# Batch by batch: an attention block and two gated MLPs on one core, with the spatial mix of the first batch moved between the attention tiles of the second

## The chip, the cores and the metric

The kernel runs on one core of a Trainium2 chip. The metric is the device time of one execution in microseconds; three runs before the change gave 393.71, 396.62 and 400.88 us, a median of 396.62 us. One execution was profiled: it took 399.25 us, of which the trace spans 396.5 us.

The engines are named as the profile names them: PE (TensorE matmul) and PEld (its weight loads), DVE (VectorE), ACT (ScalarE), POOL (GpSimd) and SP (SyncE, which here only issues DMAs). Each works through its own list of instructions in the order of that list.

## The reference

Two batches of 768 positions go through three stages. Chunked attention (8 heads of 64, chunks of 32 with 16 positions to the left, 8 to the right and 8 memory slots) gives `x` (2 x 768 x 512). A gated MLP mixes along the positions. A second MLP has a three-tap convolution along the positions.

```python
scores = q_c @ k_full.T / 8; a = softmax(scores); x = a @ v_full        # per chunk of 32
h = gelu(x @ w_in); u, v = h[..., :512], h[..., 512:]
v_n = (v - mean) / sqrt(var + 1e-6) * g_ln
v_s = einsum('ts,bsd->btd', w_sg, v_n) + b_sg[None, :, None]            # mixes positions
x2 = x + (u * v_s) @ w_out
h = relu(x2 @ w_in2)
conv = sum over k of conv_w[k] * h shifted by k - 1 positions
out = (h * sigmoid(conv)) @ w_out2
```

## The kernel before, in words

Every large product is done with fp16 halves: each operand is scaled by a power of two and split into a high and a low part, and `mm3` (line 155) sums three fp16 matmuls (high x high, high x low, low x high) in one PSUM bank. The scale comes from a bound: ACT sums absolute values (`abs_sum`, line 133), `top_of` (lines 116 to 118) transposes the sums on PE, takes their maximum on DVE, and spreads it over the partitions with a matmul against ones; `scale_from` (lines 124 and 126, DVE) makes the power of two, and `split` cuts the high part on ACT (line 141) and the low part on DVE (line 147) or POOL (lines 144 and 145). Weights arrive as 64-bit floats and are first narrowed on DVE (`narrow`, lines 103, 105 and 107).

The work is written as tokens in two strings, FIRST and SECOND; each letter is a step and its number a tile or block:

- `q i` scores of attention tile i (line 258; 12 tiles of 128 positions, six for each batch) and row maxima; `e g` the exponential of a group of tiles (line 279); `b i` transposes the weights (pp, line 285), copies them (ptr, line 288), multiplies with the values (pv, line 296), normalizes into `xx` (line 312) and bounds the result; `x i` transposes `xx` (px, line 328) and splits it.
- `c`, `s`, `k` narrow, bound and cut the eight blocks of `w_in`; `V i` and `U i` are the two halves of the first MLP (vps and ups); `N g` normalizes three tiles of v; `S` loads the mixing weights.
- `M n` is a block of the mix (group n // 4 of 384 positions; groups 0 and 1 are batch 0), `O n` the product with `w_out`, `I n` the product with `w_in2`, the convolution and the gate (n // 8 is the batch), `G b` and `H n` bound and split the gates of a batch, `Y n` the last product and the store.
- `J n` takes n jobs from a queue that holds the cutting of the later weights.

A scheduler then places the instructions on PE, DVE, ACT and POOL within the limits of buffers and data; SP keeps the order in which the program is written. Buffers come from pools: the attention's SBUF pool `at` and its PSUM pool are given back when FIRST has ended (`p1.close()`), and only then is the staging pool `st2` for the later weights opened. One `q` load has 256 KB, one tile of keys 2 x 256 KB, one of values 2 x 260 KB, and a block of `w_in` 512 KB.

## Time and profile before

| | |
|---|---|
| median of three runs | 396.62 us |
| the profiled execution, its span | 399.25 us, 396.5 us |
| busy PE, DVE, ACT, POOL | 336.8, 239.1, 218.5, 81.8 us |
| mean granted clock of TensorE | 0.914 |
| HBM read and written | 33.29 and 3.15 MB |

A busy PE is one with a matmul under way, at whichever clock was granted: 1.00 is 2.4 GHz, 0.50 is 1.2 GHz. A stretch that is busy at a lower clock holds less work than its busy time says.

### The profile page before, as it was taken

To read this page: it belongs to the slowest core of one execution; us is meant where nothing else is said; L and a number is where in the kernel's file an instruction comes from. 1 tells how busy PE (TensorE), PEld (TensorE's weight loads), DVE (VectorE), ACT (ScalarE), POOL (GpSimd) and SP (SyncE) were. 2 spreads that over 40 slices of the span, in tenths; PEclk is the share of its full clock that TensorE was granted. 3 is DMA by queue.
4 is the path that set the end of the run, shared out by engine and by line. 5 is a ranking of instruction groups with operands and counts; after the bars stand their busy time and mean duration, and the time that the engine had idled before them with its cause. 6 is when DMAs were issued, how large, how long until landed. Compare 5 with 4: busy or idle time off the path is not lost.

```text
span 396.5 us, 7270 instructions
## 1 busy us (share of the span) xinstructions
PE 336.8 (85%) x2890; PEld 211.7 (53%) x2890; DVE 239.1 (60%) x467; ACT 218.5 (55%) x439; POOL 81.8 (21%) x204
## 2 busy tenths in 40 slices
...
GB/s 221 294 312 187 159 57 211 249 105 163 119 68 69 70 0 8 194 160 2 21 144 48 108 106 2 114 100 0 3 106 0 2 54 26 28 26 28 26 79 53
DMA packets 14161, 36.89 MB, mean 93 GB/s; under 512 B 2352, under 2 KB 2608, under 8 KB 14128
## 3 DMA queue, kind: packets, MB, share of 16 engines
...
q8 instruction: 22, 0.36, 0.4%
q14 instruction: 11, 0.09, 0.1%
HBM read 33.29 MB, written 3.15 MB: 92 GB/s over the span
## 4 chain that ended last, share of the span: by engine, by line
PE 48%; DVE 17%; DMA 17%; ACT 10%; issue 4%; POOL 2%; SPq 1%; ACTq 0%; DVEq 0%; POOLq 0%
PE o L155 22%; PE i L155 7%; PE mx L155 5%; PE ups L155 4%; DMA raw<-in_w_out_dram 4%; PE vps L155 4%; DMA rvXF<-in_w_in_dram 3%; DMA ruWSG<-in_w_in_dram 3%; DMA kwb<-in_kw_dram 3%; PE sc L258 2%; DMA sgUF<-in_w_sgt_dram 2%; DVE c L690 2%; PE pv L296 2%; PE px L328 1%; ACT h L686 1%
## 5 line engine op out<-in xcount | busy, mean ns | idle before, releaser
L155 PE MATMUL o<-wp,gsp 128*128 128x512 f16 (+1 forms) x312 | 66.0, 371 | 6.9 <-ACT gsp L141 6.9
L155 PE MATMUL i<-x2s,wi 128*128 128x384 f16 x384 | 67.1, 332 | 0.2 <-ACT h L686 0.2
L155 PEld LDWEIGHTS <-wi 128*128 128x128 f16 x384 | 38.2, 100 | 27.8 <-issue 3.6
L155 PEld LDWEIGHTS <-gsp 128*128 128x128 f16 x312 | 30.9, 99 | 39.8 <-ACT gsp L141 8.0
L155 PE MATMUL mx<-wsg,vs 128*128 128x384 f16 x288 | 50.8, 333 | 0.0
L155 PE MATMUL vps<-win,xs 128*128 128x512 f16 x144 | 36.8, 400 | 4.1 <-ACT xs L141 3.8
L155 PEld LDWEIGHTS <-vs 128*128 128x128 f16 x288 | 28.3, 99 | 19.6 <-issue 2.3
L155 PE MATMUL ups<-xs,win 128*128 128x128 f16 x576 | 38.6, 225 | 0.0
L155 PEld LDWEIGHTS <-win 128*128 128x128 f16 x576 | 35.7, 101 | 4.5 <-issue 1.4
L155 PE MATMUL o<-gs,wo 128*128 128x384 f16 x192 | 34.5, 326 | 0.8 <-ACT gs L141 0.7
L690 DVE SCALAR_TENSOR_TENSOR c<-h,cw_sb,c 128x768 f32<-128x768 f32 x16 | 16.2, 1015 | 17.1 <-ACT c L689 17.1
L155 PEld LDWEIGHTS <-wo 128*128 128x128 f16 x192 | 18.5, 98 | 11.9 <-issue 0.2
L155 PEld LDWEIGHTS <-xs 128*128 128x128 f16 x144 | 13.3, 102 | 21.5 <-ACT xs L141 4.6
L361 DVE BATCH_NORM_STATS2 st<-v 128x6 f32<-128x512 f32 x12 | 8.3, 690 | 23.0 <-ACT v L359 23.0
L694 ACT ACTIVATE c<-c 128x768 f32<-128x768 f32 x16 | 13.4, 840 | 12.8 <-DVE c L692 12.8
L695 DVE TENSOR_TENSOR gate<-h,c 128x768 f32<-128x768 f32 x16 | 15.3, 955 | 8.5 <-ACT c L694 8.5
L720 ACT ACTIVATE o<-o,ixp0t 128x256 f32<-128x256 f32 x12 | 5.6, 469 | 21.8 <-issue 18.2
L133 ACT ACTIVATE gs<-uf 128x384 f16<-128x384 f32 x16 | 8.3, 519 | 16.3 <-DVE uf L652 13.8
L692 DVE SCALAR_TENSOR_TENSOR c<-h,cw_sb,c 128x768 f32<-128x768 f32 x16 | 16.2, 1015 | 0.7
L677 POOL MEMSET h<- 128x1 f32 x16 | 2.0, 129 | 68.0 <-DVE gate L695 64.2
L258 PE MATMUL sc<-kwa,q 128*32 128x128 f32 x192 | 7.9, 300 | 9.3 <-DMA kwa<-in_kw_dram 7.3
L391 POOL TENSOR_TENSOR vs<-v,vs 128x512 f16<-128x512 f32 x12 | 14.0, 1190 | 7.7 <-ACT vs L390 7.7
...
## 6 DMA issues: line engine op xcount, KB each, us to landing
...
```

The costliest lines, as they stand in the source:

```text
L133: nc.scalar.activation(room, src, AF.Abs, scale=2.0 ** (1 - EXP_TOP), accum_out=acc)
L155: nc.tensor.matmul(ps, a, b, start=(i == 0), stop=(i == n - 1))
L258: nc.tensor.matmul(sc[c * CH:(c + 1) * CH, hp].rearrange("p (a k) -> p a k", a=2), q_t[i][:, hp, c * CH:(c + 1) * CH], kw_t[i][:, :, hp, c ...
L296: nc.tensor.matmul(po[c * CH:(c + 1) * CH, hp // 2, (hp % 2) * PW:(hp % 2 + 1) * PW] .rearrange("p (a k) -> p a k", a=2), t[:, hp, c * CH: ...
L328: nc.tensor.transpose(pp[:, k * P:(k + 1) * P], x[:, k * P:(k + 1) * P], ident)
L361: nc.vector.bn_stats(out=st, in_=v)
L391: nc.gpsimd.tensor_tensor(out=lo[:, ib, :], in0=v, in1=hi[:, ib, :], op=ALU.subtract)
L690: nc.vector.scalar_tensor_tensor(out=c, in0=h[:, 0:S], scalar=cw_sb[:, f, 0:1], in1=c, op0=ALU.mult, op1=ALU.add)
L692: nc.vector.scalar_tensor_tensor(out=c, in0=h[:, 2:S + 2], scalar=cw_sb[:, f, 2:3], in1=c, op0=ALU.mult, op1=ALU.add)
L694: nc.scalar.activation(c, c, AF.Sigmoid)
L695: nc.vector.tensor_tensor(out=gate[b][f // 4][:, f % 4], in0=h[:, 1:S + 1], in1=c, op=ALU.mult)
L720: nc.scalar.activation(o[:, cs], ps[:, cs.start - cols.start:cs.stop - cols.start], AF.Copy, scale=inv_of(sc_g["gate", b], f"t{b}", f"p{h}"))
```

## The change

FIRST is reordered and a third string, B1, is added for the second batch. Its main points:

- **Loads.** Loads are tokens now (`A` q, `D` keys, `R` values, `W` blocks of `w_in`); the first tile's values, then the four blocks of the v half of `w_in`, stand ahead of tile 1.
- **Mix of batch 0.** M0 to M7 stand in B1, between the attention tiles of batch 1, and `w_out` is loaded and cut there too (`T`, into buffers outside `st2`). In SECOND the blocks of O, M and I are mixed.
- **Steps split.** `p` (pp and ptr) is taken out of `b`; `h` (the first half of a tile's bound) out of `b` and its second half goes to `x`; U is done in two halves (`u`, `w`). Scores stand some tiles ahead of their use. The groups of the exponential have one or two tiles instead of up to three.
- **Bounds in two steps.** `top_a` does the transpose and the maximum, `top_b` the matmul against ones. All bounds share one PSUM bank (`tops`, three places in turn); the spare columns of that bank take dummy matmuls (`Z`), of which there are 180 in place of 70.
- **Buffers.** Scores have one PSUM bank, pp and px two (before: four for all and for bounds), ptr has one buffer in place of two. Some low parts that POOL cut (four tiles of x, two blocks of `w_out2`) go to DVE.
- **End.** Four of the blocks of batch 0's last product, Y2 to Y5, stand after the last `I`, ahead of the second batch's product; before, Y5 alone did.

```diff
-PX = (4, 9, 10, 11)
-PK = ('p1',)
-SPMAN = True
-XBUFS, SBUFS, QBUFS, PTBUFS = 2, 2, 2, 2
+PK = ()
+QBUFS, PTBUFS, SBUFS = 2, 1, 2
 RAWBUFS = 2
-LOADS = "q0 q1 wv0 v0 wv1 v2 v1 wu0 wu1"
-GROUPS = ((0,), (1,), (2, 3), (4, 5), (6, 7, 8), (9, 10, 11))
+GROUPS = ((0,), (1,), (2,), (3, 4), (5, 6), (7, 8), (9, 10), (11,))
+SG = max(len(g) for g in GROUPS)
...
-Z q0 e0 c0 q1 e1 c1 b0 c2 c3 s0 q2 q3 e2 x0 k0 k1 k2 k3 b1 x1 c4 c5 V0 c6 c7 s1 b2 V1 x2 k4 k5 k6 k7 q4 q5 e3
-b3 V2 x3 U0 b4 V3 U1 x4 S U2 b5 V4 N0 x5 U3 q6 q7 q8 e4 V5 J2 U4 b6 J2 U5 N1 J2 x6 J2 b7 x7 J2 V6 b8 x8 U6
-V7 q9 q10 q11 e5 U7 V8 b9 x9 U8 N2 b10 x10 V9 b11 x11 U9 V10 U10 V11 U11 N3
+A0 D0 R0 W0 W1 W2 W3 A1 D1 R1
+Z70 q0 e0 A2 D2 R2 W4 W5 W6 W7 c0 p0 c1 Z30 b0 R3 c2 c3 Z60 h0 s0 x0 o0 k0 k1 k2 k3 q1 e1 A3 D3 Z20 V0 p1 q2 e2 A4 D4 b1 R4 c4 c5 p2 h1 b2 R5 c6 c7 x1 q3 A5 D5 V1 h2 s1 q4 e3 A6 D6 x2 o1 k4 k5 k6 k7 p3 U0 b3 R6
+q5 A7 D7 S0 S1 S2 V2 q6 e4 A8 D8 h3 u1 x3 p4 w1 b4 R7 J1
+V3 N0 h4 J1 u2 x4 p5 w2 b5 R8 J1
+q7 A9 D9 V4 J1 q8 e5 A10 D10 h5 u3 x5 p6 J1 w3 b6 R9 J1
+J1 V5 h6 J1 u4 x6 p7 w4 J1 b7 R10 J2
+"""
+B1 = """
+q9 A11 D11 V6 N1 q10 e6 h7 u5 x7 p8 w5 M0 b8 R11
+V7 h8 M1 u6 x8 p9 w6 b9 M2
+q11 e7 V8 h9 M3 u7 x9 p10 w7 b10 M4 g0
+V9 N2 h10 r0 T u8 x10 p11 w8 b11 M5 J1
+V10 J1 h11 M6 u9 x11 w9 J1
+V11 J1 N3 u10 J1 M7 w10 J1
+U11 g1 J3
...
 SECOND = """
-J1 M0 J1 M1 J1 M2 J1 M3 J1 M4 J1 M5 J1 M6 J1 M7 J1 M8 J1 O0 J1 M9 J1 O1 J1 M10 J1 O2 J1 M11 J1 O3 J1 M12 J1 O4 J1
-M13 J1 O5 J1 M14 J1 O6 J1 M15 J1 O7 J1 O8 J1 O9 J1 O10 J1 O11 J1 O12 I0 O13 J1 O14 I1 O15 J1 I2 J2 I3 J2 I4 J2 I5
-J3 I6 J3 I7 J3 G0 I8 H0 H1 H2 H3 I9 H4 H5 H6 H7 I10 Y0 I11 Y1 I12 Y2 I13 Y3 I14 Y4 I15 Y5 G1 H8 H9 H10 H11 H12 H13 H14
-H15 Y6 Y7 Y8 Y9 Y10 Y11
+M8 J1 r1 M9 J1 O0 J1 O1 J1 O2 J1 O3 J1 M10 J1 a0 O4 J1 O5 d0 O6 J1 O7 J1 M11 J1 a1 M12 J1 g2 d1 M13 J1 r2 J3 I0 J1 I1 M14 J1 I2 M15 J1 I3 J1 O8 g3 O9 J1 O10 r3 J1 O11 J1 I4 a2 O12 J1 O13 d2 J1 I5 O14 J1 O15 J1 I6 a3 J1 I7 d3 J1
+I8 G0 J1 I9 K0 J1 H0 H1 J1 I10 H2 H3 J2 I11 H4 H5 J2 I12 H6 H7 J2 I13 J9 Y0 I14 Y1 I15 Y2 G1 Y3 K1 H8 H9 Y4 H10 H11 Y5 H12 H13 H14 H15 Y6 Y7 Y8 Y9 Y10 Y11
...
+    pst = ctx.enter_context(tc.tile_pool(name="pst", bufs=1, space=bass.MemoryType.PSUM))
+    pst_t = pst.tile([P, 512], F32, tag="top", name="tops")
+    top_ps = pst_t[:, :3 * P + 3].rearrange("p (n c) -> p n c", n=3)
+    idle_ps = pst_t[:, 3 * P + 3:]
+    tops = [0]
...
-    small = [lambda name: ps1.tile([P, 512], F32, tag="a", name=name, bufs=4)]
-
-    def small_ps(name):
-        return small[0](name)
...
-    def top_of(m, name, ones=None):
+    def top_a(m, name):
 
         n = m.shape[1]
-        t = small_ps(name + "t")
+        tops[0] += 1
+        t = top_ps[:, tops[0] % 3]
         r = sm.tile([P, 1], BF16, tag="red", name=name + "r", bufs=4)
         nc.gpsimd.memset(r, 2.0 ** -120)
         nc.tensor.transpose(t[:n, 0:P], m, ident)
         nc.vector.tensor_reduce(out=r[:n], in_=t[:n, 0:P], axis=AX.X, op=ALU.max)
-        nc.tensor.matmul(t[:, 256:257], ones_bf if ones is None else ones, r, start=True, stop=True)
-        return t[:, 256:257]
+        return t, r
+
+    def top_b(tr, ones=None):
+
+        t, r = tr
+        nc.tensor.matmul(t[:, P:P + 1], ones_bf if ones is None else ones, r, start=True, stop=True)
+        return t[:, P:P + 1]
...
     def qk(i):
-        sc = sc_t[i] = small_ps(f"sc{i}").rearrange("p (h k) -> p h k", h=4)
+        sc = sc_t[i] = ps1.tile([P, 512], F32, tag="sc", name=f"sc{i}", bufs=1).rearrange("p (h k) -> p h k", h=4)
         for hp in range(4):
             for c in range(4):
                 nc.tensor.matmul(
...
                     kw_t[i][:, :, hp, c, :],
                     start=True, stop=True,
                 )
-        load_qk(i + 2)
...
+        pp = ps1.tile([P, 512], F32, tag="a", name=f"pp{i}", bufs=2)
...
-        if i in PX:
-            nc.scalar.copy(xf[b][:, :, ts], ppv)
-        if i in sc_x:
-            split(xs[b][0][:, :, ts], xs[b][1][:, :, ts], ppv, sc_x[i], xf[b][:, :, ts] if i in PX else None)
-        if i not in PX:
-            nc.scalar.copy(xf[b][:, :, ts], ppv)
+        split(xs[b][0][:, :, ts], xs[b][1][:, :, ts], ppv, sc_x[i])
+        nc.scalar.copy(xf[b][:, :, ts], ppv)
...
+    def u_pe(i, part):
         b, ib = divmod(i, KS)
         sl = slice(ib * P, (ib + 1) * P)
-        ps = ps_t["u", i] = mmps1(f"ups{i}").rearrange("p (j q) -> p j q", j=KD)
-        for j in range(KD):
+        if part == 0:
+            ps_t["u", i] = mmps1(f"ups{i}").rearrange("p (j q) -> p j q", j=KD)
+        ps = ps_t["u", i]
+        for j in (2 * part, 2 * part + 1):
...
+                if n == 0:
+                    raw_t["o"] = big.tile([P, 2, DM], src.dtype, tag="WI1", name="rawo")
+                raw_t[n] = raw_t["o"][:, n % 2:n % 2 + 1]
+            else:
+                raw_t[n] = late_pool[0].tile([P, ks.stop - ks.start, cs.stop - cs.start], src.dtype, tag="raw",
+                                             name=f"raw{n}", bufs=RAWBUFS)
...
+    def warm(n):
+
+        for _ in range(n):
+            nc.tensor.matmul(idle_ps, ones_bf, ones_bf[:, :idle_ps.shape[1]], start=True, stop=True)
...
+    def bound(kind, g):
+        acc_t[kind, g] = top_a(acc_t[kind, g], f"{kind}{g}")
+
+    def scaled(kind, g):
+        sc_g[kind, g] = scale_from(top_b(acc_t.pop((kind, g))), f"{kind}{g}")
...
+    def wo_jobs():
+        def get():
+            late["wo"] = [big.tile([P, KD, DM], F16, tag=t, name=f"wo{t}") for t in ("WO0", "WO1")]
+            return late["wo"]
+
+        stage_jobs("o", w_out, KD, slice(0, DM), get)
+        issue(0)
+        issue(1)
+
+    steps["M"] = lambda n: mix(n // KD, n % KD)
+    steps["T"] = lambda n: wo_jobs()
+    steps.update({
+        "g": lambda n: bound("gs", n), "r": lambda n: scaled("gs", n), "a": lambda n: bound("x2", n), "d": lambda n: scaled("x2", n)})
+    run(B1)
+    p1.close()
+    late_pool.append(ctx.enter_context(tc.tile_pool(name="st2", bufs=1)))
+    tp = ctx.enter_context(tc.tile_pool(name="tp", bufs=2))
+    ps2.append(ctx.enter_context(tc.tile_pool(name="ps2", bufs=7 - PS_MM, space=bass.MemoryType.PSUM)))
```

Three places on PE. First, what stands ahead of V0 (`vps_463` before, `vps_464` in the change); sc, px, pp and pv are an attention tile's scores, transposes and products, wvt and tops the bounds, and a wait names the engine or DMA queue it is for. Before:

```order
L118 MATMUL wvt<-wvr,ones_bf 128x1 [waits DVE_49]
L258 MATMUL sc_337<-kwa,q_233 32x128 [waits DMAHW6_49,DMAHW7_49,DMAHW0_49,PE_49]
...
L258 MATMUL sc_362<-kwb,q_263 32x128 [waits DMAHW2_49,DMAHW3_49,DMAHW1_49,PE_49]
...
L328 MATMUL px_387<-ident,xx 128x128 [waits DVE_49]
...
L285 MATMUL pp_406<-ident,s_269 128x128 [waits DVE_49]
...
L155 MATMUL vps_463<-win_107,xs_307 128x512
```

Now:

```order
L343 MATMUL px_395<-ident,xx 128x128 [waits DVE_49]
...
L273 MATMUL sc_492<-kwa,q_232 32x128 [waits DMAHW6_49,DMAHW0_49,DMAHW7_49,DVE_49,PE_49]
...
L125 MATMUL tops<-ident,wav 4x128 [waits DVE_49]
L299 MATMUL pp_485<-ident,s_437 128x128 [waits Activation_49]
...
L310 MATMUL pv_518<-vwSTG,ptr_490 32x130 [waits DMAHW5_49,DMAHW4_49,Activation_49]
...
L132 LDWEIGHTS ones_bf [waits DVE_49]
L132 MATMUL tops<-wvr,ones_bf 128x1 [waits Pool_49]
L299 MATMUL pp_551<-ident,s_511 128x128 [waits PE_49,Activation_49]
...
L533 MATMUL tops<-ones_bf 128x125 [waits DVE_49]
```

V0 stood behind the scores of tiles 2 and 3 (`sc_337`, `sc_362`); now it stands behind those of tile 2 alone (`sc_492`), tile 1's product with the values, the bound of the weights and 20 dummies. The transpose for the weights' bound (`wav`), whose data ACT makes, now also waits for DVE.

Second, PE around V7 in batch 1. Before, between the product with the values of tile 8 and the next transpose stood V and U alone:

```order
L296 MATMUL pv_1468<-vwSTG_95,ptr_1466 32x130 x16
...
L155 MATMUL vps_1563<-win_107,xs_1266 128x512
...
L155 MATMUL ups_1649<-xs_1266,win_107 128x128
...
L116 MATMUL xt8t<-ident,xa_1491 1x128
L328 MATMUL px_1502<-ident,xx 128x128 x4
L258 MATMUL sc_1583<-kwb,q_1129 32x128 x16
```

Now:

```order
L310 MATMUL pv_1642<-vwSTG_98,ptr_1587 32x130 x7
...
L169 MATMUL mx_0_1618<-wsg_820,vs_1018 128x384
...
L169 MATMUL vps_1667<-win_112,xs_1307 128x512
...
L343 MATMUL px_1743<-ident,xx 128x128 x4
L299 MATMUL pp_1751<-ident,s_1464 128x128 x2
L125 MATMUL tops<-ident,xa_1663 1x128
...
L169 MATMUL mx_1_1691<-wsg_820,vs_1018 128x384
...
L169 MATMUL ups_1714<-xs_1307,win_112 128x128
```

A block of the mix (18 matmuls, `mx_0`, `mx_1`) now stands between a tile's product and its transposes, and another between its transposes and U.

Third, PE at the end, from the last `I` (i_7 of batch 1) to batch 1's first block of the last product (`o_0_0_4055` before, `o_0_0_4127` in the change). Before:

```order
L155 MATMUL i_7_3976<-x2s_2952,wi_2512 128x384
...
L155 MATMUL o_5_0_3997<-wp_3007,gsp_3520 128x512
...
L116 MATMUL gt1t<-ident,gacc_3526 16x128
L118 LDWEIGHTS ones_low
L118 MATMUL gt1t<-gt1r,ones_low 128x1
...
L155 MATMUL o_0_0_4055<-wp_3007,gsp_4034 128x512
```

Now:

```order
L169 MATMUL i_7_3962<-x2s_3173,wi_2621 128x384
...
L169 MATMUL o_2_0_3983<-wp_3242,gsp0XS_3634 128x512
...
L125 MATMUL tops<-ident,gacc_3545 16x128
...
L169 MATMUL o_3_0_4016<-wp_3242,gsp0XS_3634 128x512
...
L132 MATMUL tops<-gt1r,ones_low 128x1
...
L169 MATMUL o_4_0_4057<-wp_3242,gsp0XS_3634 128x512
...
L169 MATMUL o_0_0_4127<-wp_3242,gsp1XS_4048 128x512
```

One block of 24 matmuls stood between the last `I` and the gates' bound; now four blocks stand between the last `I` and batch 1's last product, one ahead of each step of the bound and two behind it.

## Rows read from the trace of the kernel before

**Rows 1.** Stretches: length, busy PE, PEld, DVE, ACT, POOL, SP; clock; DMA share; GB/s

```profile
0.00:41.40 41.40, 18.23 (x247) 14.91 (x248) 24.40 (x47) 12.53 (x28) 19.55 (x31) 0.65 0.92 252
41.40:104.00 62.60, 52.35 (x729) 38.92 (x730) 28.69 (x75) 37.86 (x58) 14.41 (x50) 0.93 0.59 156
104.00:172.00 68.00, 55.40 (x681) 39.19 (x680) 33.10 (x81) 36.38 (x62) 17.95 (x48) 0.87 0.26 74
172.00:293.00 121.00, 120.01 (x778) 72.84 (x777) 103.15 (x208) 78.59 (x192) 20.58 (x51) 1.00 0.21 70
293.00:312.00 19.00, 11.65 (x55) 5.72 (x53) 17.62 (x24) 17.05 (x32) 8.15 (x10) 0.73 0.00 0
312.00:353.00 41.00, 41.00 (x216) 21.02 (x215) 21.14 (x22) 21.14 (x45) 0.80 (x12) 1.00 0.09 33
353.00:361.00 8.00, 6.04 (x29) 2.69 (x28) 4.34 (x7) 4.90 (x9) 0.33 (x2) 0.99 0.08 33
361.00:396.50 35.50, 32.17 (x166) 16.42 (x164) 6.68 (x8) 10.04 (x18) 0.00 (x0) 0.95 0.12 45
```

**Rows 2.** Timeline up to V0: start, us, engine, line, operation; idle time before it

```profile
16.32 1.96 PE L296 MATMUL pv<-vwa,ptr 128*32 128x130 f32 x32 [0.98 <-ACT ptr L288]
...
25.54 0.43 DVE L103 TENSOR_SCALAR tuVS<-ruWSG 128x512 int32<-128x512 int32 x1 [2.47 <-DMA ruWSG<-in_w_in_dram]
...
29.23 1.66 POOL L144 TENSOR_SCALAR tvXS<-tvXS,wvs 128x512 f32<-128x512 f32 x1
...
34.64 1.94 PE L258 MATMUL sc<-kwa,q 128*32 128x128 f32 x32 [7.34 <-DMA kwa<-in_kw_dram]
...
34.87 2.79 POOL L145 TENSOR_TENSOR win<-tvXS,win 128x512 f16<-128x512 f32 x2
...
37.55 1.94 PE L258 MATMUL sc<-kwb,q 128*32 128x128 f32 x32 [0.97 <-DMA kwb<-in_kw_dram]
...
41.38 3.72 PE L155 MATMUL vps<-win,xs 128*128 128x512 f16 x12
```

**Rows 3.** Waits of the attention stage and of bounds: engine, line, waited for

```profile
PE pv L296 <- ACT ptr L288: 7.4, 7, 2.0
PE xt0t L116 <- ACT xs L133: 5.6, 1, 5.6
PE xt0t L118 <- DVE xt0r L117: 2.5, 1, 2.5
PE wp1t L118 <- DVE wp1r L117: 1.7, 1, 1.7
PE gt1t L118 <- DVE gt1r L117: 0.7, 1, 0.7
```

**Rows 4.** Groups by line: busy us, mean ns of one, idle time before

```profile
L650 DVE SCALAR_TENSOR_TENSOR mt<-mx,gsc,b_sb 128x384 f32<-128x384 f32 x16 | 9.6, 607 | 1.5 <-POOL vs L391 0.9 <-PE mx L155 0.6
L652 DVE TENSOR_TENSOR uf<-mt,uf 128x384 f32<-128x384 f32 x16 | 9.1, 568 | 0.1
L528 PE MATMUL warm<-zero 128*128 128x128 f16 x70 | 6.4, 278 | 1.0 <-DVE zero L525 1.0
L279 ACT ACT_TABLE_LOAD x4 | 5.1, 1283 | 0.8 <-PEq L796 0.7
```

**Rows 5.** Timeline: the mix at full clock, and the gates of both batches

```profile
184.83 7.80 PE L155 MATMUL mx<-wsg,vs 128*128 128x384 f16 x47
...
304.89 1.03 PE L155 MATMUL o<-wp,gsp 128*128 128x512 f16 x2 [5.64 <-ACT gsp L141]
...
360.15 7.52 DVE L147 SCALAR_TENSOR_TENSOR gsp<-gate,gt1s,gsp 128x768 f16<-128x768 f32 x8 [0.81 <-ACT gsp L141]
360.18 33.00 PE L155 MATMUL o<-wp,gsp 128*128 128x512 f16 x168 [1.22 <-ACT gsp L141]
```

**Rows 6.** Chain that ended last: start, us, what; the batch-1 block in between

```profile
339.78 3.90 PE i L155 x24
343.68 5.18 PE o L155 x24
```

More of the change, by code (lines that the diff above doesn't have):

```diff
@@ L232, in fused_kernel, with load_q @@
     q_t, kw_t, vw_t = {}, {}, {}
+    def load_q(i):
+        q_t[i] = at.tile([P, 4, P], F32, tag="q", name=f"q{i}", bufs=QBUFS)
+        nc.sync.dma_start(q_t[i], qt[i])
     def load_halves(t, src):
@@ L432, in fused_kernel, with sg_load @@
     sg_t = []
-    def sg_load():
-        wsg.extend(halves("wsg", ("WSG0", "WSG1"), KS, S))
-        for tag, ks in (("UF1", slice(0, 2)), ("UF1", slice(2, 4)), ("VS10", slice(4, 6))):
-            if ks.start != 2:
-                t = big.tile([P, 4 if tag == "UF1" else 2, S], F32, tag=tag, name=f"sg{tag}")
-            sg_t.append(t[:, ks.start % 4:ks.start % 4 + 2])
-            nc.sync.dma_start(sg_t[-1], blocks(w_sgt)[:, ks])
+    def sg_load(n):
+        if n == 0:
+            wsg.extend(halves("wsg", ("WSG0", "WSG1"), KS, S))
+            t = big.tile([P, 4, S], F32, tag="UF1", name="sgt0")
+            sg_t.extend((t[:, 0:2], t[:, 2:4]))
+        elif n == 2:
+            sg_t.append(big.tile([P, 2, S], F32, tag="VS10", name="sgt2"))
+        nc.sync.dma_start(sg_t[n], blocks(w_sgt)[:, 2 * n:2 * n + 2])
+        if n == 2:
+            nc.sync.dma_start(g_sb, g_ln.rearrange("(k p) -> p k", p=P), allow_slow_non_contiguous=True)
+            nc.sync.dma_start(b_sb, b_sg.unsqueeze(0).to_broadcast([P, S]))
+            nc.sync.dma_start(cw_raw, conv_w)
+            sg_jobs()
     def sg_jobs():
```

175 lines of the change are left out of this document (58 added, 117 removed).

## The prediction

> **What bounds the kernel now.** I read the stretches first [rows 1]. PE is busy 336.8 of 396.5 us, so the question is where it is not, and there are four such places. Up to 41.4 us it waits for the first data and does 18.23 us at clock 0.65. From 41.4 to 172, the attention with the first MLP, it is busy 52.35 of 62.6 and 55.40 of 68.0 us at clocks 0.93 and 0.87. From 172 to 293 it is gapless at full clock. Around 293 to 312, the first batch's gates, it has 11.65 of 19 at 0.73, and around 353 to 361, the second batch's gates, 6.04 of 8. So there are two kinds of loss, idle time and the slower clock that goes with it. I count both: length less busy time times clock is 13.9 + 19.8 = 33.7 us in the attention stage, of which 10.25 + 12.6 = 22.9 is plain idle, and 10.5 us at the first gates. Matmul records can be missing and a mean clock covers idle time too, so I take 27 for the attention stage, between 22.9 and 33.7.
>
> Whose fault the idle time is, the waits say [rows 3]. Seven products with the values wait for ACT's copy of the weights (7.4 us), and one bound waits 5.6 us for ACT. No engine is full there: in the two halves DVE has 28.69 and 33.10 us and ACT 37.86 and 36.38 [rows 1]. PE is held by the latency of each tile's chain over ACT and DVE, with too little other work in its list between the links. Work put between the links is therefore free, as long as ACT and DVE keep up.
>
> **Start: -5 us (between -8 and +3).** V0 starts at 41.38 and runs 3.72 [rows 2], so it ends at 45.1. Ahead of it PE waits for the keys of tile 2 until 34.64 and of tile 3 until 37.55 [rows 2]. Ahead of tile 2's keys came three q, keys and values and all of `w_in`: 3 x 256 + 3 x 512 + 3 x 520 + 8 x 512 = 7960 KB. Now it is three q and keys, two values and four blocks: 768 + 1536 + 1040 + 2048 = 5392 KB. At the stretch's 252 GB/s [rows 1] the old amount takes 32.3 us, so the first 2.3 us are empty, and the new amount lands at 2.3 + 21.9 = 24.2. Tile 3's keys are no longer ahead of V0 at all. What is late next is the weights. Their three pieces on POOL, subtract 1.66 and narrow 2.79 for two, ran from 29.23 to 34.87 + 2.79 = 37.66 [rows 2], 8.4 us. In the new order the weights' bound on PE stands behind scores of tile 2 (1.94), tile 1's transposes and its products with the values (1.96) [rows 2], and on DVE behind the first narrowing of the u half (at 25.54 before). I let the bound end at 31, a little later than the 29.23 of before; POOL ends at 39.4, and V0, which takes pieces as they come, at 40. If the bound comes at 29 or earlier it is -8; if tile 2's exponential holds the list, +3. The 20 dummies directly ahead of V0 end before POOL's first piece: 110 more dummies at 6.4 / 70 = 0.091 us each [rows 4] are 10 us of PE, all before V0 where PE has 41.4 - 18.2 = 23.2 us idle. Cover gone, the last 20 would cost 1.8.
>
> **Attention stage: -17 us (between -28 and -7).** Eight blocks of the mix move here. 47 matmuls took 7.80 us [rows 5], so a block of 18 takes 2.99 and eight take 23.9. They leave the gapless stretch, where each of their microseconds counted in full, and stand where PE is idle. The DVE work of a block, 0.607 + 0.568 [rows 4], is 9.4 us for the eight, and the load, narrowing and cutting of `w_out` come too. U in halves and scores emitted tiles ahead give more pieces to put between the links. Against it: one score bank and one ptr buffer in place of shared four and two, so the next scores wait for the exponential that reads the bank, and the next copy for the last product. If ACT's 74.2 us of this stage [rows 1] stay (a few copies change), it has room in what remains, but not everywhere. The loss was 27; all of it filled leaves about 6 for the clock after short waits, the chain's waits halved leaves 16; I take 10, nearer the low end since the blocks stand at the links that waited. The ends are 6 - 33.7 and 16 - 22.9.
>
> **First gates: -6.5 us (between -9.6 and 0).** PE waits 5.64 us for the first split [rows 5], and the clock falls. Eight splits take DVE 7.52 us in the second batch [rows 5]. Before, three blocks I of 3.90 [rows 6] stood between the bound and the last product, 11.7 us; now five, 19.5. The 7.8 us more would remove most of 10.5. But DVE was busy 103.15 of 121 and then 17.62 of 19 [rows 1], and when 23.9 us of PE and only 9.4 of DVE leave, DVE has 93.8 against PE's 96. I keep 4 lost.
>
> **Second gates: -4 us (between -4 and -1).** The idle part is 8 - 6.04 = 1.96 [rows 1]. The last 168 matmuls take 33.00 [rows 5], while six blocks at 5.18 [rows 6] are 31.1: 1.9 of slow clock. Now three blocks, 15.5 us, stand behind the bound's start in place of none; the eight splits take 7.5 and the bound 1 to 2. Both items go.
>
> **Added: +2 us (between 0 and +10).** Four to five more table loads, as groups of the exponential get smaller: the order has 13 for 9, four at 1.283 [rows 4], 5.1 us of ACT, hidden in its slack of 130.6 - 74.2. Six cuts that POOL did go to DVE (a wider one, of 768 columns, takes 7.52 / 8 = 0.94 there [rows 5], so 5.6 us at most), four of them in this stage, where DVE is busy 61.8 of 130.6. Cover gone in either, the whole amount counts.
>
> **Sum:** -5 - 17 - 6.5 - 4 + 2 = -30.5. The profiled execution took 399.25 and its span 396.5, so 2.75 lie outside, and that stays. 399.25 - 30.5 = 368.75; this execution is 2.6 above the median, from which it would be 366.1. I say **367 us**.
>
> **Rivals.** *PE gapless after V0 (352 us).* Busy time times clock after 41.4 adds up to 303.0 over the rows [rows 1]; V0 would start 5 earlier at 36.4, 3.3 follow the last matmul (360.18 + 33.00 to 396.5 [rows 1, 5]), 2.75 lie outside: 345.4, and 6.7 more since I took 27 for 33.7. For it: all four losses are addressed. Against: every link still passes two engines.
>
> *The attention stage loses as much as before (384).* One score bank and one ptr buffer tie the tiles more closely than two and four did; the seven waits for ptr [rows 3] would become a wait in nearly every tile. The 17 do not come. Against it: the blocks of the mix depend on no tile of batch 1.
>
> *DVE bounds the second half (376).* DVE's 93.8 + 17.62 + 1.5 for cuts from POOL are 113 before the first gates' splits end, PE's part 96 + 11.65 x 0.73 = 104.5. Then 8.5 are lost where I kept 4, and the later splits and bounds, which queue on DVE, lose as much again: +9. For it: DVE is at 85% before, and PE's part shrinks more. Against: `w_out`'s narrowing leaves too.
>
> *Slower: the shared bank of the bounds.* All 30 bounds now use one PSUM bank. Each step on it, transpose and product, waits for DVE to have read the step before, and behind it stands all of PE's list. The order shows it: the weights' transpose, whose data come from ACT, now also waits for DVE. PE's second steps waited for the maximum 2.5, 1.7 and 0.7 at most [rows 3], the others no longer than the last, so 0.16 on average over 30 if those three were all; at that price 60 steps are 10, partly already paid. The most expensive row, 2.5, would give 150. At 0.36 us per step the gain is within 2% (367 + 21.6 = 388.6); from 0.63 per step, 37.8 us, it is slower (404.8). For it: DVE is loaded, and its list is in order. Against: the other half of the change puts other work between the two steps, so that the maximum is long done. The Trainium skill, *PSUM — Partial Sum Buffer*, section "PSUM bank collisions raise a hardware error", says to guard PSUM by semaphores by bank (and by quadrant of partitions), not by address: by that rule three places in one bank do not make three bounds independent. No row of before shows a bank shared by bounds in this way, and by that rule alone this rival stands and has its waits, not its price.
>
> **Numbers.** Forecast 0.58, gapless 0.13, DVE 0.13, attention unchanged 0.08, shared bank 0.08 (half of it within 2%, half slower). The forecast's own terms spread by about 10 either way. 8 in 10 lie from 351, the gapless case, to 387, which takes in DVE and the unchanged attention. 2% of 396.62, about what a measurement here tells from no change, puts "same" at 388.7 to 404.6. The shared bank and the tails of the two middle rivals give 0.07 same and 0.05 slower; the rest, 0.88, is faster.
>
> **What would show it.** V0 starts at 36 to 38 with POOL as its last wait; the keys of tile 2 land near 24. From V0 to the first O, PE idles 12 us or less, at a clock above 0.95. M0 to M7 have no waits of their own. No gap over 3 us at the first split of batch 0, none at the second batch's last product. I am wrong if ACT or DVE is over 90% busy in the attention stage with PE idle (the chain, not the fill, bounds), if steps on the bounds' bank (L125, L132) head PE's waits with more than 10 us, or if V0 starts after 41.

## The result, and the profile after

The changed kernel takes **380.5 us** (median of 378.60, 378.82, 382.17 and 383.01), the kernel before 397.9 beside it: a ratio of 0.960, 95% interval 0.948 to 0.972. It is faster by 17 us, where 30 were forecast; the range (351 to 387) holds it. Its profiled execution is the one of 383.01 us, with a span of 381.2, at the upper end of its runs as that of before was of its own, so spans are compared with spans: 15.3 us less.

Busy time by stretch (columns as in [rows 1]), of the kernel before, cut at other times than there:

```profile
42.00:96.00 54.00, 44.71 (x618) 31.95 (x617) 25.02 (x68) 33.62 (x55) 11.89 (x37) 0.96 0.58 156
96.00:119.00 23.00, 18.56 (x229) 14.93 (x230) 12.44 (x29) 14.96 (x23) 6.36 (x20) 0.78 0.39 101
119.00:168.00 49.00, 39.87 (x544) 29.07 (x543) 21.19 (x57) 23.60 (x39) 14.11 (x41) 0.91 0.24 67
```

The same stretches of the changed kernel:

```profile
42.00:96.00 54.00, 42.33 (x541) 29.12 (x540) 27.44 (x67) 36.57 (x54) 10.48 (x32) 0.84 0.62 167
96.00:119.00 23.00, 19.85 (x320) 15.31 (x323) 14.77 (x37) 16.57 (x25) 5.75 (x22) 1.00 0.45 107
119.00:168.00 49.00, 46.02 (x465) 30.68 (x460) 32.90 (x76) 26.28 (x57) 10.10 (x35) 1.00 0.24 77
```

Busy time times clock is the work done at full speed. From 119 to 168 it rises from 36.3 to 46.0 us: that is where the blocks of the mix now stand. From 96 to 119, before the first of them, it rises too, from 14.5 to 19.9. From 42 to 96, the first batch's attention, it falls from 42.9 to 35.6; PE is busy only 2.4 us less there, and the rest is the granted clock, 0.84 for 0.96. The change loses at the start of the stage and wins behind it.

Summed up from the start in pieces of 6 us, without the dummies, this gives the work done by a time, and the difference of two kernels is a lead that can be followed. Three of the experiments below have the changed kernel's order on every engine until well past 192 us (tail put back, cuts on POOL, spread splits) and a fourth (less narrowing) until about 165, so their profiles repeat its first half. I call these four the siblings:

```
work done (us at full clock) by     42    72    96   120   144   168   192   240   288
kernel before                      7.4  29.9  50.7  65.8  84.6 101.7 124.9 172.7 220.1
changed kernel                    12.9  32.7  49.2  70.0  94.0 115.0 136.5 183.9 229.4
  its lead                        +5.5  +2.8  -1.5  +4.2  +9.4 +13.3 +11.6 +11.2  +9.3
same first half, tail put back    14.3  35.4  52.6  74.8  98.8 119.2 142.0 189.4 233.6
same first half, spread splits    12.7  34.3  52.1  74.7  98.7 119.3 141.7 189.0 233.1
same first half, cuts on POOL     14.3  35.2  54.3  76.8 100.8 121.4 143.8 191.2 236.3
same first half, less narrowing   13.6  34.5  52.2  72.5  96.5 117.3 141.3 188.7 236.7
mix put back                      13.7  34.6  52.1  73.3  93.1 109.4 133.4 180.8 226.3
```

The profiled execution of the changed kernel is behind the four siblings, by 5 to 7 us of work at 192. The pattern is the same in all: 5 to 7 ahead at 42, most of that gone at 96, then 13 to 20 at 168.

Some of what PE waits for in the changed kernel, engine and line, then us in total, times, longest (answers to [rows 3]):

```profile
PE pv L310 <- ACT ptr L302: 6.7, 3, 4.4
PE sc L273 <- DMA kwb<-in_kw_dram: 4.9, 3, 2.1
PE tops L132 <- DVE wp1r L126: 3.2, 1, 3.2
PE tops L125 <- DVE x23s L138: 2.2, 1, 2.2
PE i L169 <- ACT h L663: 1.4, 1, 1.4
```

The wait for ptr comes three times instead of seven, and is hardly shorter in sum (6.7 us for 7.4). The places, from PE's timeline (start, us, engine, line, operation; idle time before it), for [rows 2] and [rows 5]:

```profile
40.12 0.59 PE L169 MATMUL vps<-win,xs 128*128 128x512 f16 x2 [0.49 <-POOL win L159]
...
72.89 1.96 PE L310 MATMUL pv<-vwSTG,ptr 128*32 128x130 f32 x32 [4.41 <-ACT ptr L302]
...
119.35 2.45 PE L169 MATMUL mx<-wsg,vs 128*128 128x384 f16 x14
...
302.58 0.18 PE L132 MATMUL tops<-wp1r,ones_bf 128*128 128x1 bf16 x1 [3.24 <-DVE wp1r L126]
304.15 3.61 PE L169 MATMUL i<-x2s,wi 128*128 128x384 f16 x12 [1.39 <-ACT h L663]
307.60 2.75 PE L169 MATMUL o<-wp,gsp0XS 128*128 128x512 f16 x12
```

V0's last piece ends at 40.7. The largest gap of the first batch is at 68 to 73 us, and the first block of the mix starts at 119. The first gates still cost a gap, at 299 to 304; the second batch's product follows the first's at 346.6 without one (PE is busy in all of the 70.31 us from 307.60 on, as a row below shows).

From V0's start to the first O, of the kernel before and of the changed one (columns as above):

```profile
41.38:199.41 158.03, 134.98 (x1606) 95.24 (x1606) 81.42 (x198) 86.95 (x153) 38.93 (x117) 0.92 0.38 104
34.27:192.46 158.19, 136.18 (x1621) 93.55 (x1619) 99.45 (x224) 95.04 (x172) 39.85 (x114) 0.95 0.45 121
```

The stretch is as long as before, and PE idles 22.0 us in it for 23.1.

### The profile page after: what moved, and what is told of

It reads as the page before. It is cut to its first block, busy times and chain, and to the rows that moved or that the text cites. A ratio compares the mean times of both kernels' runs of the same rounds, so it can differ in the third digit from the quotient of the medians.

```text
span 381.2 us, 7494 instructions
## 1 busy us (share of the span) xinstructions
PE 338.9 (89%) x3000; PEld 214.9 (56%) x3000; DVE 241.9 (63%) x472; ACT 221.8 (58%) x445; POOL 63.5 (17%) x192
## 4 chain that ended last, share of the span: by engine, by line
PE 55%; DMA 18%; DVE 14%; ACT 4%; POOL 3%; SPq 2%; issue 2%; ACTq 0%; DVEq 0%; POOLq 0%
PE o L169 25%; PE i L169 10%; PE mx L169 7%; PE vps L169 4%; DMA kwb<-in_kw_dram 3%; DMA cw_raw<-in_conv_w_dram 3%; DMA raw<-in_w_in_dram 3%; DMA rvXF<-in_w_in_dram 3%; DMA kwa<-in_kw_dram 2%; PE ups L169 2%; PE sc L273 2%; PE pv L310 2%; DMA q<-in_qt_dram 2%; SPq L256 2%; DMA raw<-in_w_out_dram 1%
## 5 line engine op out<-in xcount | busy, mean ns | idle before, releaser
L169 PEld LDWEIGHTS <-vs 128*128 128x128 f16 x288 | 27.2, 98 | 20.6 <-issue 1.9
L169 PE MATMUL o<-gs,woWO 128*128 128x384 f16 x192 | 32.4, 326 | 0.0
L169 PEld LDWEIGHTS <-woWO 128*128 128x128 f16 x192 | 18.6, 98 | 12.1
L402 POOL TENSOR_TENSOR vs<-v,vs 128x512 f16<-128x512 f32 x12 | 15.0, 1259 | 10.8 <-ACT vs L401 10.8
L169 PE MATMUL o<-wp,gsp1XS 128*128 128x512 f16 (+1 forms) x84 | 16.7, 349 | 0.0
L169 PE MATMUL o<-wp,gsp1VS 128*128 128x512 f16 (+1 forms) x84 | 16.7, 349 | 0.0
L169 PE MATMUL o<-wp,gsp0VS 128*128 128x512 f16 x72 | 16.7, 379 | 0.0
L169 PE MATMUL o<-wp,gsp0XS 128*128 128x512 f16 x72 | 16.5, 379 | 0.0
L310 PE MATMUL pv<-vwSTG,ptr 128*32 128x130 f32 x256 | 11.2, 312 | 5.2 <-ACT ptr L302 5.1
L283 DVE TENSOR_REDUCE mx<-sc 128x8 f32<-128x512 f32 x12 | 8.2, 687 | 11.9 <-PE sc L273 11.8
```

The lines of the kernel that those rows point to most:

```text
L169: nc.tensor.matmul(ps, a, b, start=(i == 0), stop=(i == n - 1))
L283: nc.vector.tensor_reduce(out=mx, in_=scv, axis=AX.X, op=ALU.max)
L310: nc.tensor.matmul(po[c * CH:(c + 1) * CH, hp // 2, (hp % 2) * PW:(hp % 2 + 1) * PW] .rearrange("p (a k) -> p a k", a=2), t[:, hp, c * CH: ...
L402: nc.gpsimd.tensor_tensor(out=lo[:, ib, :], in0=v, in1=hi[:, ib, :], op=ALU.subtract)
```

## The experiments

Each starts from the changed kernel. Ratios are to the kernel before, run beside them, with the 95% interval in brackets. Each version's interval is about 0.8% either way, so a difference of 3 us or less between two versions is told by the rows of their profiles or not at all. Diffs show the changed pieces of a line; `...` and `/` stand for what is left out.

**Load order undone.**

```diff
-... q0 e0 A2 D2 R2 W4 W5 W6 W7 c0 ...
+... q0 e0 W4 W5 W6 W7 A2 D2 R2 c0 ...
```

> The changed kernel with one thing undone: the four blocks of the u half of w_in stand ahead of tile 2's q, keys and values again. Theory (the new load order is worth about the 4.5 us by which V0 ends earlier): tile 2's keys land 2048 KB / 252 GB/s = 8.3 us later, at 33 to 34 us in place of 25.6; V0 ends at 45 or later in place of 40.65; the whole takes 4 to 6 us more, about 385. Rival (what V0 gains is lost again in the first batch's attention, whose chains end when the later loads and ACT let them): V0 ends later but the first block of the mix starts at about the same 119 us; the whole takes 380 to 382.

Measured: 382.6 us, 0.967 (0.959 to 0.975). From PE's timeline, the scores of tile 3, V0's last piece and the first block of the mix:

```profile
38.63 1.07 PE L273 MATMUL sc<-kwb,q 128*32 128x128 f32 x30 [2.04 <-DMA kwb<-in_kw_dram]
...
41.67 0.60 PE L169 MATMUL vps<-win,xs 128*128 128x512 f16 x2
...
120.21 2.92 PE L169 MATMUL mx<-wsg,vs 128*128 128x384 f16 x17 [0.59 <-ACT uf L418]
```

V0 ends at 42.3 and not at 45. Tile 2's scores run 6.5 us later than in the change (32.05 for 25.59), but seven of V0's twelve matmuls are placed around them, from 33.9 to 36.5. The last five stand behind the scores of tile 3, for whose keys PE waits until 38.63; POOL's pieces were done at 37.45. So V0's end hung on keys here, but on tile 3's. The mix starts 0.9 later than in the changed kernel, and the 2 us are within what the runs scatter. The rival is nearer, and the load order is worth at most these 2.

**The mix put back.**

```diff
-... w5 M0 b8 / h8 M1 u6 / b9 M2 / h9 M3 u7 / b10 M4 g0 / h10 r0 T / b11 M5 J1 / h11 M6 u9 / J1 M7 w10 / U11 g1 J3 ...
+... w5 b8 / h8 u6 / b9 / h9 u7 / b10 / h10 T / b11 J1 / h11 u9 / J1 w10 / U11 J3 ...
-M8 J1 r1 M9 ...
+M0 M1 M2 M3 M4 g0 M5 r0 M6 M7 g1 M8 J1 r1 M9 ...
```

> The changed kernel with M0 to M7 (and the bounds and splits of their two groups) put back behind the attention, ahead of M8; the load and cutting of w_out stay in the attention. Theory (the blocks fill idle time of batch 1's attention, 119 to 192 us, which lost about 5 us with them and 19.8 in the kernel before without): idle time of PE in the second half of the attention rises by 10 to 15 us, and the whole takes 390 to 395. Rival (the finer order of the other steps has closed those gaps by itself, and the blocks could stand anywhere): the stage gets shorter by the 24 us of the blocks, the rest longer by the same, and the whole stays at 379 to 382.

Measured: 387.7 us, 0.979 (0.973 to 0.986), 7 more than the change; its four runs (387.06 to 388.25) lie above all of the change's. The stretches, columns as above:

```profile
96.00:119.00 23.00, 20.20 (x310) 15.50 (x307) 16.48 (x41) 17.20 (x26) 6.82 (x23) 1.00 0.42 106
119.00:168.00 49.00, 39.76 (x437) 28.78 (x435) 29.70 (x75) 27.76 (x54) 11.08 (x33) 0.93 0.31 99
```

Work from 119 to 168 is back at 37.0, near the 36.3 of before: the finer order closed no gap there, the blocks did. From 96 to 119 it is 20.2 without any block, for 14.5 before: that part of the gain is not the mix's. So filling is the largest single part of the gain that an experiment shows, 7 of 17 us, though below the 10 to 15 that I put on it.

**The tail put back.**

```diff
-... I13 J9 Y0 I14 Y1 I15 Y2 G1 Y3 K1 H8 H9 Y4 H10 H11 Y5 H12 ...
+... I13 J9 Y0 Y1 I14 Y2 Y3 Y4 I15 Y5 G1 K1 H8 H9 H10 H11 H12 ...
```

> The changed kernel with Y2 to Y4 put back between the last I blocks, so that Y5 alone stands between the last I and the second gates' bound, as in the kernel before. Theory: the chain of the second gates shows again, 2 us of idle time and some 2 us of slower clock: 4 us more, about 384.5. Rival (those blocks now fill gaps between the last I blocks, where PE waits for h and for the first gates' splits): the gap near 300 us gets shorter by about as much, and the whole stays at 380 to 381.

Measured: 381.8 us, 0.965 (0.958 to 0.973). The waits are back, as in [rows 5] for the kernel before:

```profile
342.00 0.18 PE L132 MATMUL tops<-gt1r,ones_low 128*128 128x1 bf16 x1 [0.75 <-DVE gt1r L126]
343.40 8.12 PE L169 MATMUL o<-wp,gsp1XS 128*128 128x512 f16 x31 [1.22 <-ACT gsp1XS L155]
```

The change behind its first gates' gap, in two stretches (columns as above):

```profile
304.15:307.60 3.45, 3.45 (x13) 1.62 (x13) 2.54 (x6) 3.45 (x9) 0.28 (x3) 0.55 0.00 0
307.60:377.91 70.31, 70.31 (x363) 35.24 (x361) 25.62 (x30) 31.29 (x62) 0.86 (x10) 1.00 0.11 43
```

The second of them with the tail put back:

```profile
302.10:376.40 74.30, 72.33 (x364) 35.68 (x361) 27.33 (x32) 33.35 (x65) 0.86 (x10) 0.98 0.11 41
```

From the first gates' product to the last matmul it takes 74.3 us where the change takes 70.3: 4.0 more, in kind and in size the theory. The median shows only 1.3 of it. In the two profiles the first gates cost less here, though the edit changes nothing ahead of them: their two waits are 2.7 us (1.30 and 1.39) for 4.6 in the change (3.24 and 1.39), and the twelve matmuls behind them take 1.94 us at a granted clock of 1.00 for 3.45 at 0.55.

**Bounds in one step.**

```diff
         nc.vector.tensor_reduce(out=r[:n], in_=t[:n, 0:P], axis=AX.X, op=ALU.max)
+        nc.tensor.matmul(t[:, P:P + 1], ones_bf if ones is None else ones, r, start=True, stop=True)
         return t, r
...
         t, r = tr
-        nc.tensor.matmul(t[:, P:P + 1], ones_bf if ones is None else ones, r, start=True, stop=True)
```

> The changed kernel with each bound's two steps on PE emitted together again (transpose, maximum, product with ones), on the same shared bank. Theory (the steps must be apart, since PE stands still while DVE, which is loaded, gets to the maximum): the 30 second steps wait 0.3 to 0.6 us each more, PE's waits at the product with ones rise from 5.2 us to 12 or more, and the whole takes 6 to 14 us more, 387 to 394. Rival (a scheduler places the second step freely, and apart from the text of the order nothing changes): within 2 us of 380.5. Second rival (what costs is the shared bank): fewer bounds are open at once, and the whole gets faster by 2 to 4.

Measured: 381.4 us, 0.964 (0.958 to 0.971). This is the first rival: taking the steps apart is worth nothing that can be measured. PE is no later at 288 (234.8 of work) but then waits longer for h, the output of `I` that goes into the gate:

```profile
302.21 3.77 PE L169 MATMUL i<-x2s,wi 128*128 128x384 f16 x12 [5.62 <-ACT h L663]
```

**Less narrowing on DVE.**

```diff
         nc.vector.tensor_scalar(out=d, in0=hi, scalar1=3, scalar2=0x3FFFFFFF,
                                 op0=ALU.logical_shift_left, op1=ALU.bitwise_and)
+        if light:
+            return
...
-            narrow(self.t(self.pieces[j]), self.raw(j))
+            narrow(self.t(self.pieces[j]), self.raw(j), self.key[0] in "ip")
```

> The changed kernel, where DVE's narrowing of w_in2 and w_out2 leaves out two of its three operations (so these weights keep a few bits only; all else is computed as before). In the stretch from the first block O to the first gates' product (192.5 to 304.2 us) that takes 24 operations of 0.68 us off DVE, some 16 of its 98.6. Theory (DVE is the floor of this stretch: 98.6 busy of 111.7, and PE loses 7.7 there): the loss falls to 2 to 4, and the whole takes 374 to 377. Rival (the loss is the latency of the gates' own chain over ACT and DVE, whatever DVE's load): the stretch keeps its 111 to 112 us, and the whole takes 379 to 382.

Measured: 376.3 us, 0.948 (0.943 to 0.952). The time is the theory's, the place is not. Work from 192 to 288 is 95.4 us of 96, where the changed kernel and the other siblings do 91 to 93, so DVE's load cost 2 to 4 us there. But the gap at the gates stays:

```profile
297.90 3.48 PE L171 MATMUL i<-x2s,wi 128*128 128x384 f16 x12 [5.09 <-ACT h L665]
```

**The same, with bounds in one step.** Both edits above.

> The same narrowing left out, and the bounds' two steps emitted together (the run with that alone took 381.4 us, though PE was some 5 us of work ahead at 288 us; it lost that in a wait of 5.6 us for h near 302). Theory (DVE's floor took that lead away): with DVE relieved the lead stays, and the whole takes 368 to 373, 2 to 6 less than with the narrowing alone. Rival (the lead was lost to the gates' chain): 379 to 382 again, or the same as with the narrowing alone.

Measured: 378.5 us, 0.952 (0.946 to 0.958). A miss for the theory: a wait of 4.5 us for h is there again. DVE's load is not what makes it.

**The first batch's order.**

```diff
-q5 A7 D7 S0 S1 S2 V2 q6 e4 A8 D8 h3 u1 x3 p4 w1 b4 R7 J1
+q5 A7 D7 V2 h3 u1 x3 p4 w1 b4 R7 q6 e4 A8 D8 S0 S1 S2
```

> The changed kernel with two pieces of the first batch's order moved: the loads of the mixing weights (and so ACT's sums over them, one of which held ACT's list 4.3 us for its DMA at 64 to 68 us) behind tile 8's keys, and the scores and the exponential of tiles 5 and 6 behind tile 4's transposes, so that ACT copies tile 4's weights first. Theory for the first batch's attention (its largest gap, 4.4 us at 68 to 73 with the slow clock behind it, is ACT's list and not ACT's load): that gap goes, and the first block of the mix starts at 114 to 116 us in place of 119.4. Theory for the whole (DVE is the floor behind it): only 0 to 2 us of that arrive, 378 to 381. Rival (there is no such floor): all of it arrives, 375 to 377. Second rival (the gap opens at the next load): the mix starts at 118 to 121 and the whole stays.

Measured: 380.0 us, 0.958 (0.953 to 0.964). The first block of the mix:

```profile
111.59 3.08 PE L169 MATMUL mx<-wsg,vs 128*128 128x384 f16 x18 [0.68 <-ACT v L370]
```

In the changed kernel ACT's list around the gap at 68 to 73 reads:

```profile
68.42 1.48 ACT L147 ACTIVATE wsg<-sgt 128x1536 f16<-128x1536 f32 x1 [4.29 <-DMA sgt<-in_w_sgt_dram]
...
71.31 1.06 ACT L293 ACTIVATE s<-s 128x1024 f32<-128x1024 f32 x1
72.27 0.57 ACT L302 COPY ptr<-pp 128x512 f32<-128x512 f32 x1
```

With the other order the gap is gone, so it was ACT's list, where tile 4's copy stood behind sums that waited for a DMA and behind an exponential. The mix starts 2.5 to 7.8 us earlier than in the siblings and the change (114.1 to 119.4), but by 192 us the work done is 141.0, theirs 141.3 to 143.8 and the change's 136.5. From 119 to 192 PE is busy 66.1 us at 0.95, so the lead is spent before the stretch in which I expected it to be lost.

**Cuts moved to POOL.**

```diff
-PK = ()
+PK = ('i1','p0',)
```

> The changed kernel with the low parts of the second half of w_in2 and the first half of w_out2 cut on POOL, eight pieces of 0.74 us taken off DVE and some 2.7 us each put on POOL, which is busy 9.8 of 111.7 us in that stretch; everything is computed. Theory (DVE is the floor): 6 us less on DVE gives 1.5 to 4 us, 376.5 to 379. Rival (POOL's pieces come late for I4 and the products, or slow DVE down beside them): 380 to 384, with PE waiting for POOL.

Measured: 391.3 us, 0.983 (0.975 to 0.990): 10 to 11 more, worse than the rival said. PE's longest wait, then DVE and POOL around the first gates:

```profile
PE i L169 <- ACT h L663: 9.0, 3, 4.0
```

```profile
279.36 1.01 DVE L669 SCALAR_TENSOR_TENSOR c<-h,cw_sb,c 128x768 f32<-128x768 f32 x1
280.29 1.51 DVE L161 SCALAR_TENSOR_TENSOR x2s<-xf,x23s,x2s 128x384 f16<-128x384 f32 x1
281.73 0.61 DVE L161 SCALAR_TENSOR_TENSOR x2s<-xf,x23s,x2s 128x384 f16<-128x384 f32 x1
282.26 1.91 DVE L161 SCALAR_TENSOR_TENSOR gsp0XS<-gate0UF,gt0s,gsp0XS 128x768 f16<-128x768 f32 x1
284.09 1.00 DVE L161 SCALAR_TENSOR_TENSOR gsp0XS<-gate0UF,gt0s,gsp0XS 128x768 f16<-128x768 f32 x1
...
291.54 0.94 DVE L672 TENSOR_TENSOR gate0XF<-h,c 128x768 f32<-128x768 f32 x1
```

```profile
279.45 1.94 POOL L159 TENSOR_TENSOR wp<-tp,wp 128x512 f16<-128x512 f32 x1
...
281.81 1.54 POOL L159 TENSOR_TENSOR wp<-tp,wp 128x512 f16<-128x512 f32 x1
...
292.55 0.10 POOL L654 MEMSET h<- 128x1 f32 x1 [9.19 <-DVE gate0XF L672]
```

The first split takes 1.91 us beside POOL's subtraction and the next 1.00 after it; with three operations before it DVE loses some 2.7 us in this way between 276 and 284. The gate operation that gives h back comes behind all eight splits. How the rest of the 10 to 11 us comes about was not separated. The order on DVE suggested a ring for the next run: a gate operation gives an h buffer back, it stands behind the splits on DVE, and until it has run ACT can write no new h.

**The first gates' splits spread.**

```diff
+        sc = sc_g["gate", b]
+        n = (None, None, 1, 1, 2, 2, 3, 3)[f]
+        if b == 0 and n is not None:
+            sc = sm.tile([P, 1], F32, tag=f"gl{f}", name=f"gl{f}")
+            nc.vector.scalar_tensor_tensor(out=sc, in0=gacc[1][:, 2 * n + 1:2 * n + 2], scalar=0.0,
+                                           in1=sc_g["gate", b][:, 0:1], op0=ALU.mult, op1=ALU.add)
+        split(gsp[b][0][f // 4][:, f % 4], gsp[b][1][f // 4][:, f % 4], gate[b][f // 4][:, f % 4], sc)
```

> The changed kernel with the first gates' splits spread: the splits of blocks 2 and 3 take a copy of the scale that depends on block I9's sum, those of 4 and 5 on I10's, those of 6 and 7 on I11's (six small operations more on DVE, values unchanged). Theory (the gap near 300 us is a ring: eight splits in a row on DVE, 7.7 us, stand ahead of the gate operation that gives an h buffer back, so ACT's next h waits, the PSUM banks stay full and PE stops): PE's gap at 299 to 304 us falls from 4.8 to 2 or less, the stretch from the first block O to the first gates' product from 111.7 to 106 to 109 us, and the whole takes 375 to 378. Rival (DVE's whole load is the floor, wherever the splits stand): the stretch keeps its 111 to 112, the whole 379 to 382. Second rival (the last split now comes late for the product): a wait of PE at the first block of the last product, 382 to 385.

Measured: 377.4 us, 0.956 (0.948 to 0.963). DVE in the changed kernel, where the low parts of the splits stand in a row (290.5 to 298.6) and the gate follows at 302.45; then ACT, with the high parts and the h behind the gate:

```profile
290.50 1.02 DVE L161 SCALAR_TENSOR_TENSOR gsp0XS<-gate0UF,gt0s,gsp0XS 128x768 f16<-128x768 f32 x1
...
292.03 2.88 DVE L161 SCALAR_TENSOR_TENSOR gsp0XS<-gate0UF,gt0s,gsp0XS 128x768 f16<-128x768 f32 x3
294.82 3.81 DVE L161 SCALAR_TENSOR_TENSOR gsp0VS<-gate0XF,gt0s,gsp0VS 128x768 f16<-128x768 f32 x4
298.54 1.95 DVE L667 SCALAR_TENSOR_TENSOR c<-h,cw_sb,c 128x768 f32<-128x768 f32 x2
...
302.45 0.94 DVE L672 TENSOR_TENSOR gate1UF<-h,c 128x768 f32<-128x768 f32 x1
```

```profile
287.47 3.40 ACT L155 ACTIVATE gsp0XS<-gate0UF,gt0s 128x768 f16<-128x768 f32 x4
290.78 3.40 ACT L155 ACTIVATE gsp0VS<-gate0XF,gt0s 128x768 f16<-128x768 f32 x4
...
303.42 0.58 ACT L663 ACTIVATE h<-i,ixi0x 128x384 f32<-128x384 f32 x1 [0.21 <-DVE gate1UF L672]
```

With the splits spread, DVE and PE:

```profile
294.71 1.81 DVE L672 TENSOR_TENSOR gate1UF<-h,c 128x768 f32<-128x768 f32 x2
```

```profile
307.23 1.32 PE L169 MATMUL o<-wp,gsp0VS 128*128 128x512 f16 x4 [0.50 <-DVE gsp0VS L161]
309.53 2.11 PE L169 MATMUL i<-x2s,wi 128*128 128x384 f16 x12 [0.99 <-ACT o L703]
```

DVE does the same work and a little more, its gate operation comes 3.3 us earlier counted from the first O, and PE's 4.6 us of waits at the gates (3.24 and 1.39) fall to 1.5 (0.50 and 0.99). So the order of the splits holds the gate and h up: the ring is there. Its size and its engine are less sure. The edit spreads both parts of a split, and in the change ACT's eight high parts stand in a row too, from 287.5 to 294.2, with the next h behind them; which of the two rows holds PE was not separated. And the gap varies with the splits in a row: the run below without the added dummies has waits of 1.30 and 1.39 us there. From the first O to the last matmul it takes 185.4 us in the change, 183.7 in that run and 182.8 here, so the spread is worth 1 to 3 us. My stretch of 111.7 us ended at 304.15 with an I block, not with the gates' product; to the first matmul of that product it is 115.1 in the change and 112.3 here (187.97 to 300.30): 2.8 less, where 3 to 6 were forecast, and twelve matmuls of an I block stand behind that first matmul here and ahead of it in the change.

**The added dummies taken out.**

```diff
-... p0 c1 Z30 b0 R3 c2 c3 Z60 h0 ... D3 Z20 V0 ...
+... p0 c1 b0 R3 c2 c3 h0 ... D3 V0 ...
```

> The changed kernel without its 110 added dummies (70 are left at the start). Theory (they stand where PE has nothing else, and cost nothing; what they give is the clock): the clock granted to the first V is lower or as low as now, V0 ends 0 to 2 us later, and the whole is within 2 us of 380.5. Rival (the 20 directly ahead of V0 hold it up, 2.2 us): V0 ends 1 to 2 us earlier, and the whole takes 378 to 379.

Measured: 378.3 us, 0.959 (0.950 to 0.968). The scores of tile 3, the last five matmuls of V0, and the wait at the first gates:

```profile
38.86 1.94 PE L273 MATMUL sc<-kwb,q 128*32 128x128 f32 x32 [4.46 <-DMA kwb<-in_kw_dram]
...
45.65 1.25 PE L169 MATMUL vps<-win,xs 128*128 128x512 f16 x5
...
298.40 0.18 PE L132 MATMUL tops<-wp1r,ones_bf 128*128 128x1 bf16 x1 [1.30 <-DVE wp1r L126]
```

V0 ends at 46.9, 6 us later where the theory allowed 2, and later than before the change. The mix starts at 117.2, within the siblings' spread, and the kernel is no slower. The clock fell as the theory has it: from 25 to 41 us it is 0.53, with the dummies 0.71. But the scheduler also puts tile 3's scores ahead of V0 then, and PE waits 4.46 us for their keys, so the 6 us are not the clock's alone.

**Spread splits and the other order.** The two edits together.

> The spread splits and the first batch's pieces in the other order (loads of the mixing weights behind tile 8's keys, tile 4's copy ahead of the exponential; that alone started the mix at 111.6 us in place of 119.4 and took 380.0 us in the whole). Theory (the ring at the first gates took that lead away): with the ring open both gains add, and the whole takes 372 to 376. Rival (what was gained in the first batch's attention is lost again in the second batch's, before the first block O): the same as with the spread alone, within 1.5 us.

Measured: **375.7 us**, 0.952 (0.943 to 0.960); all four runs (373.96 to 378.24) lie below the lowest of the change. The mix starts early and the work at 192 is 143.5, no more than the best sibling's. It is 1.7 below the spread alone, which does not tell theory from rival.

**That, without the added dummies.** The three edits together.

> Spread splits, the other order of the first batch's pieces, and no added dummies (70 at the start). Theory (the start is off the path: without the dummies alone V0 ended 6 us later and the whole was no slower, 378.3): the same as with spread and order, 375.7, within 1.5 us, though V0 ends 4 to 6 us later. Rival (now that the first batch's attention has lost its largest gap, its chains begin at V0, and the start counts): 378 to 381. Second rival (the dummies hold PE's list up): 372 to 374.

Measured: 386.2 us, 0.982 (0.976 to 0.987): the first rival, and more than it asked for. PE's longest wait:

```profile
PE sc L273 <- DMA kwb<-in_kw_dram: 12.1, 4, 4.6
```

V0 ends at 45.9 where it ends at 39.5 with the dummies, and the mix starts 10 us later (120.7 for 110.7). Without them the scheduler also places ACT's and DVE's early work in another order, and PE waits 12.1 us for keys, 4.6 of them for tile 3's ahead of V0; with the dummies it is 3.0 in all. How much of the 10.5 us is the start and how much this order was not separated.

## Why the prediction was right in sign and too large

The leads of the profiled execution over the kernel before are 5.5 us up to 42 us, 6.1 from there to 192, 2.2 from 192 to 318 and 3.7 behind it; the terms were 5, 17, 6.5 and 4. (The leads add up to 17.5 where the spans differ by 15.3: in all, 2.2 us more work is counted for the changed kernel, so they are no sharper than that.)

**Start, -5:** V0 ended 4.4 us earlier, at 40.7 where 40 was forecast, and by the wait forecast (POOL), but the term was put on the path, and there it does not lie: with V0 back at 42.3 or 46.9 the time moved by +2 and -2. The first batch's attention takes the lead back (5.5 to -1.5 between 42 and 96). This holds for the change's order: in the best order, taking the dummies away ended V0 6 us later and cost 10, of which the start's share is open.

**Attention stage, -17: the step that failed.** The lead grew by 6.1 between 42 and 192 us in the profiled execution and by 10 to 12 in four siblings. From V0 to the first O PE idles 22.0 us, where 12 or less were forecast and the kernel before idles 23.1. The sum set eight blocks of the mix against the loss of the whole stretch of 41 to 172 us. But M0 needs all six tiles of batch 0 normalized, and starts at 114 to 119. It fills the second batch's half, where the work rises by 9.7 us in 49, and cannot reach the first half. There PE is held by the chains over ACT, by a list of ACT that waits for the mixing weights and, in the siblings, by the next keys, and the new order does 3 to 7 us less from 42 to 96 than the old one. The 5.7 that it wins back from 96 to 120 come without the mix. Filler is worth what the gaps hold that it can reach: 7 us here.

**First gates, -6.5:** the cover of five blocks in place of three was there, but the splits run as soon as their data are there, whatever stands between them in the string, and on ACT and DVE they hold up the gate that frees h. The waits are 4.6 us for 7.3 before (1.7 [rows 3] and 5.64 [rows 5]), and 2.2 for `x23s` came in. Of the 6.5, 2.2 came in the profiled execution and 3.8 with the tail put back; with the splits spread it is 4.7 (lead from 192 to 318). The DVE rival (376) had one of the two engines and the wrong reason: it is the order of the work more than DVE's sum, of which 2 to 4 us show.

**Second gates, -4:** right in kind and in size. No wait is left there; the experiment that undoes it costs 4.0 behind the first gates.

**Added, +2:** not to be seen apart.

**The shared bank:** its waits are there and small. All that stand at its steps (L125 and L132), whatever they wait for, sum to 9.5 us for 60 steps, 0.16 each; in the kernel before, the same steps (L116 and L118) on the shared four banks had 20.0. Emitted together the steps cost nothing more. No run gives the bounds their banks back, so the bank's own price stays open. The Trainium skill, *PSUM — Partial Sum Buffer*, section "PSUM bank collisions raise a hardware error", asks that accesses to one bank be kept apart by semaphores, and that part agrees with the waits for DVE in the order; it has no price.

The two rivals with a smaller gain, 376 and 384, both lie nearer to 380.5 than the 367 of the forecast. The range holds the result because its upper end was drawn to take them in, which is no merit of the sum. Neither came as it was written: the waits for ptr are three, not one in nearly every tile, and relieving DVE left the gates' gap. Put back one at a time, the mix costs 7 us, the load order at most 2 and the tail 1 to 4; the remaining 4 to 7 of the 17 no run assigns to a part of the change.
